# Attention, gate and channel block: 64-bit weights converted in chunks of 512 columns, with a new written order of jobs

## The chip, the cores and the metric

One core of a Trainium2 chip runs the whole block. The metric is the device time of one execution in microseconds (us). Three runs of the kernel before gave 603.58, 603.62 and 603.73 us; the median is 603.62 us. One further execution was profiled. PE is the matmul engine (PEld its weight loads), DVE the vector engine, ACT the scalar engine, POOL the GpSimd engine, SP the engine that issues most DMAs.

## What is computed

Three stages follow each other, for 2 batches of 768 tokens of 512 channels:

```
mask = bucket(q) == bucket(k)                      # hashed with a small projection
a    = softmax(where(mask, q @ k.T / 8, -1e9)) @ v # 8 heads of 64
g    = sigmoid(causal_conv5(a, conv_w)) * (a @ w_val) @ w_out
u    = g + real(fft(fft(g, axis=seq), axis=channel))
out  = u + relu(layernorm(u) @ w_ch1) @ w_ch2
```

The weights w_val, w_out, conv_w, w_ch1 and w_ch2 arrive as 64-bit floats. The kernel takes their bits apart with integer operations and makes of each number two 32-bit parts, a high and a low one, which the matmuls then use as separate products.

## The kernel before, in words

The attention works on 8 pairs of heads. Each pair has 6 query tiles for each of its two heads, so there are 96 steps, numbered n from 0. `ATTENTION` (lines 116 to 408) has one string of jobs for each step; `follow` (line 719) issues them in exactly that order, and the engines run their own instructions in the order of issue. A job's name may carry + or -, which shift the step that it belongs to: `X++` in the string of step 10 is the X of step 12. The jobs of a step are:

- C (PE, line 982): scores, 128 queries x 768 keys, into the one score bank; c (DVE, 992) clamps them into SBUF and takes a minimum.
- X (ACT, 1001): Exp; T (PE, 1012): six transposes; H (ACT, 1024) copies them as the high part; L (DVE, 1027) makes the low part.
- V (PE, 1038): product with the values; O (ACT, 1045) takes the sum out, o (SP) moves half of it across partitions, A (POOL, 1064, "xm") adds the halves.
- et, eh, el, J0, J1, S, s, z, Q0, b0 and others prepare the next pairs. P (POOL, 631 and 633) are steps of the convolution, two for each tap.
- w0 to w7 convert w_val, u0 to u7 the first chunk of w_out. In the last steps E (PE, 614) are the first products with w_val, sg0 to sg3 (ACT, 604) the sigmoids of the gate, and wm (1368) a Sigmoid of one column.

`words_split` (line 654) gives the eight steps of a conversion. a0 and g0 (DVE) mask the high word of a number; g1 joins the low word to g; a1 (ACT) rescales the exponent; a2 (DVE) puts the sign back; e0 (DVE) takes the power of two out of a; low (DVE) multiplies g by it; high (ACT) copies a. Before, a unit of work is half a chunk: 128 rows x 256 columns (`half_weights`). Words a and g lie side by side in one PSUM bank, the bank "m", and word e lies in SBUF, in the buffer "cve". Each of the 8 pairs converts one half of w_val (four chunks of 128 rows), and the last pair also converts the two halves of w_out's chunk 0. SP loads a half (256 columns of 64 bits) into one of two buffers `wvr`. Chunks 1 to 3 of w_out are converted behind the attention by `chunk` (line 1633), already by 512 columns, with a in the bank "m", g in the bank "o" and e in SBUF.

The weights of the channel stage go through another function, `from64` (line 502), by 512 columns; its words all lie in SBUF. Its lines 525, 532 and 538 are the counterparts of a0, g0 and g1.

A second list, `ORDERS` (line 37), has the order of the jobs of the stages behind the attention.

Of the kernel before, what the change touches and what calls it, by code (L numbers as in the profile page):

```python
# [10 lines left out]
F32 = mybir.dt.float32  # L11
# [3 lines left out]
I32 = mybir.dt.int32  # L15
I64 = mybir.dt.int64

P = 128
# [20 lines left out]
O8 X7a D6a X7b O9 H7a O10 Y8 L7a H7b E8 A6a st1 Y9 B6a L7b E9 st0 X8a Y10 X9a D7a st3 H8a D7b ag3 st4 A7a O11  # L39
ag0 L8a sq0 A7b ag1 ag4 H9a sq1 L9a rs0 st5 no3 E10 no0 st2 D8a ag5 Y11 ag2 B7a D9a sq2 B7b A8a rs1 X10a B8a A9a  # L40
r0 H10a E11 r3 no4 L10a D10a B9a no1 rs2 X11a r4 v0 r1 H11a w0 v3 no2 L11a D11a w3 A10a r2 v1 B10a N00 no5 w1
A11a c32 r5 c30 B11a N10 v5 c36 v4 Z00 v2 c31 w2 N01 Z10 w4 N11 P00 w5 N02 P10 st0+ Z01 N12 c33 Z11 c35 c38 I0a
c37 P01 st3+ Z12 P11 I0b st1+ h0a l0a c40 c34 c41 I1a st4+ h0b c43 c47 ag3+ ag0+ c42 sq0+ I1b c45 Z02 h1a c46
# [4 lines left out]
ur0 c54 S14 uc0 T0++ c55 tr1 ag5 T1++ S11 sq2 tc1 c60 ur1 bh0 rs2 c62 I2a bl0 c61 uc1 c66 no5 S12 c63 no2 I2b  # L48
c67 c68 h2a c64 c65 l2a c72 ta0 tr2 c70 h2b S20 tc2 l2b c71 S24 W1+ S23 c73 c76 ur2 S22 W2+ uc2 c78 c77 bh2 I3a
# [3 lines left out]
I0a td0- td2- tb1- A2 te2- td1- I0b A6 h0a th2- te1- l0a f0 F3 tl2- h0b th1- G0 f2 I1a te0- l0b A0 tl1- F1 T2+  # L53
h1a F5 f3 W6 F4 l1a A1 T3+ G2 f5 I1b f1 f4 A3
# [3 lines left out]
M5 T7 s1 F5 s3 B3- F1 U1+ B5- B8- M3 B7- B4- M7 l11 A2 U0+ G2 c12 F4 c22 h12 W1 G1 h22 W2 M4 W3 A0 F0 W4 A1 l22  # L58
""",
    """  # L60
M1 h21- U2 W5- l21- W6- G0- l12- G5- U3 s0 A6- G3- W7- M2 T0 M6 A3- c11 G4- A5- A8- A7- s1 F3 T1 A4- F2 B0- M5
T2 B1- T3 B2- M7 s3 B3- h11 T4 B5- F1 B6- F0 B7- B8- T5 F4 l11 T6 c22 M3 U4 B4- G0 A0 c12 F5 T7 h12 M4 h22 A1
# [3 lines left out]
M1 h21- l21- G4- U5- s0 l22- U6- F0 A2- A3- G3- A7- A5- G1- U7- F1 G2- A6- B0- M2 A8- A4- B1- B2- M6 c11 B3- F3  # L66
s1 B7- F2 f0 B6- M5 f2 B8- G5- f3 s3 B5- M7 f1 h11 B4- M3 c22 W0 M4 l11 A0 c12 F5 h21 A2 F4 W1 h22 f5 G2 h12 f4
""",
    """
M1 W2- l21- G0- s0 l22- A1- G1- W3- W4- F0 l12- A3- M2 W5- A6- W6- G4- A7- A8- G5- A5- W7- F1 M6 c11 A4- M5 s1  # L70
B2- B0- h11 B1- F2 l11 s3 M7 B3- B6- B5- M3 B7- B8- A0 B4- G3- A1 G2 A3 F3 c12 A5 A2 h12 F5 A7 c22 F4 l12 M4 A6
B0 A8 A4
""",
    """
M1 h21- h22- l21- G0- l22- s0 B1- B2- F2 B3- G5- W0- B5- M2 B6- G4- B7- B8- B4- G1- A2 F0 W1- F1 A6 W2- M6 A0
W3- A1 c11 G3- f1 h11 M5 s1 A3 f0 A8 F3 s3 f2 F5 W4- M3 W5- l11 W6- A7 M7 f3 A5 c12 G0 c22 h12 G2 f5 W7- F4
# [3 lines left out]
l11 A2 A3 G0 s1 l22- A5 M5 A7 A6 M7 B0 A8 A4 B1 G5- W0 s3 F3 B3 c22 F1 B5 B2 M3 F4 c12 B7 M4 h12 A0+ l12 A1+ G1  # L80
B6 F5 A3+ B8 h22 B4 G2 h21 G4 l21 A2+ G3 W1
""",
    """
M1 W2- W3- M2 s0 W4- A7 W5- F0 A6 W6- M6 l22- A8 A5 A4 F1 c11 s1 B2 G5- B0 W7- B1 M5 B6 M7 s3 f1 h11 F2 c22 F5
# [3 lines left out]
M1 B5- B7- f3- G2- A0 B4- M4- A1 l12- A2 G5- h21- A3 G1- l21- A5 A7 F2 s0 f4- G0- A6 G4- A4 A8 F0 l22- B0 F1 W0  # L88
# [5 lines left out]
A0+ f1 F3 A1+ M6 h11 f3 A2+ F2 A3+ s1 A6+ M5 A5+ A7+ A8+ f0 M7 s3 l11 A4+ M3 c22 f2 G0 c12 F4 B0+ f5 G1 B1+ B2+  # L94
h12 G2 B3+ h22
# [3 lines left out]
M5 l11 W2 W3 F4 s3 W4 A6+ M7 W5 A7+ G2 B0+ A4+ F5 B1+ M3 B2+ W6 c22 B3+ F0 B7+ G0 c12 M4 G1 h21 h22  # L99
# [18 lines left out]
T Y0 Y1 y0 H C+++ y1 X++ R+ c+++ yz  # L118
""",
    """  # L120
T r L- C+++ U- yb- H X++
""",
    """
T c++ cl-- L- X++ C+++ wl0-- V q- H D2-- c+++ wl+++++ R
""",
    """
T r- L- C+++ X++ q- V H c+++ R O
""",
    """
T r- k0-- o- L- U+++ C+++ X++ Q0 q- V H c+++ R  # L130
""",
    """
T r- L- A-- C+++ H q- V k1--- c+++
""",
    """
T O- X+ k3---- o- J0- k2---- k7---- J1- L- D0---- C+++ S- H V s- c+++ X++ z- J0 J1 L
""",
    """
T S- C+++ s- H k6----- V z- c+++ X++
""",  # L140
    """
T A--- b0-- L- O- X++ C+++ k4------
""",
    """
T w0-- H- o-- w1-- et c++ V- D1------- k5------- eh H V w2-- L- w3-- C+++ X++ k8-------
""",
    """
T A--- c++ O- et o- eh L- C+++ X++ Q1- el- H c+++
""",
    """  # L150
T et w4---- C+++ L- w7---- A-- H V- ns-- c+++ eh V el- X+++ C++++ w5---- L
""",
    """
T O- X+ o- V w6----- el- b1--- H c+++ k9----------
""",
    """
T et L- C+++ eh D0+ H V c+++ A-- X++
""",
    """
T L- C+++ O- X++ o- el- et V c+++ D1 eh  # L160
""",
    """
T H- k10------------- np- C+++ L- H V X++ A-- el- J0+ c+++ et O
""",
    """
T o- L- et C+++ Q0- eh eh- V c+++ H J1 X++ V+ el- L A- C++++ S U----- X+++ s
""",
    """
T c+++ J0 H J1
""",  # L170
    """
T O- L- z-- S- o- C+++ X++ el-- s- V D2------ c+++ H z-
""",
    """
T b0-- L- C+++ H V c+++ X++ A--
""",
    """
T L- O- C+++ o- H w0-- U--- V nr- X++ w1-- c+++
""",
    """  # L180
T w3--- et L- C+++ H A-- w4--- V eh c+++ U++
""",
    """
T O- X+ L- o- et C+++ Q1- el- eh V H w5---- nm c+++
""",
    """
T X+ et L- C+++ H ns-- el- V A-- eh c+++
""",
    """
T P0- O- X+ L- o- C+++ P0-- b1--- V H el- c+++ P0 w7------  # L190
""",
    """
T X+ w2------- D2- C+++ L- wl------- et V c+++ eh H
""",
    """
T w6-------- A--- O- et L- X+ C+++ P0 o- el- V H D0 c+++
""",
    """
T eh- X+ el- et D1- C+++ L- H V A-- c+++ eh
""",  # L200
    """
T P0- O- X+ np-- o- el- J0 C+++ L- Q0- H U+ J1 c+++
""",
    """
T S- X+ et- s- V- L- J0 H A-- C+++ eh- z- L X++ J1 V c+++ S
""",
    """
T O- s- X++ o- C+++ z-
""",
    """  # L210
T H- c++ P0--- b0-- V- L- X++ C+++ P0-- w0- wl- V H c+++ el---
""",
    """
# [2060 lines left out]
```

## Time and profile before

| | before |
|---|---|
| median of 3 runs | 603.62 us (603.58 to 603.73) |
| the profiled execution | 603.55 us |
| its span, first to last instruction | 601.7 us |
| around the span | 1.85 us |
| DVE busy | 527.4 us (88%), 1042 instructions |
| ACT busy | 377.7 us (63%), 750 instructions |
| POOL busy | 228.3 us (38%) |

The granted clock of PE is full speed (2.4 GHz) in all of the span. The attention's transposes run from 13 to 240 us; its last products end near 251 us. PE has work in nearly every microsecond from there to the end. In the views, "idle before" names the wait of an engine ahead of an instruction and what ended it; times of the timeline count from the start of the span. Matmul ends are modelled, so the weight loads tell more about gaps than the matmuls.

### The profile page before, as it was taken

What the parts mean: (1) busy time and instruction counts of PE and PEld (TensorE: products, weight loads), DVE (VectorE), ACT (ScalarE), POOL (GpSimd) and SP (SyncE); (2) the same over time, 40 slices, a digit from 0 to 9 for tenths busy, and PEclk for the clock granted to TensorE, in tenths of its full rate; (3) what the DMA queues carried; (4) which work ended last, traced back from release to release, by engine and by line L of the source; (5) the groups of instructions that cost most, each with busy time, mean ns of one, the idle gap of its engine ahead of it and who ended that gap; (6) DMA issues with size and microseconds to landing.
All of it is one profiled execution on the core that took longest, in us unless ns stands there. A gap on an engine that the chain in (4) does not pass through costs nothing.

```text
span 601.7 us, 10402 instructions
## 1 busy us (share of the span) xinstructions
PE 591.5 (98%) x3631; PEld 540.8 (90%) x3631; DVE 527.4 (88%) x1042; ACT 377.7 (63%) x750; POOL 228.3 (38%) x272
## 2 busy tenths in 40 slices
PE   8999999999999999999999999999999999999997
PEld 6889999999999989998899989999989898889886
DVE  5998999999999998799789999999999999985335
ACT  6898999998999987853636465545353443442121
POOL 7422769696989797894340310000000000000000
PEclk9999999999999999999999999999999999999999
DMA  5866686757575651144021122112232232310004
GB/s 131 210 144 138 164 203 152 191 132 180 154 164 150 176 130 45 45 177 164 1 71 36 36 71 70 36 35 71 71 96 80 70 101 76 104 36 0 2 35 175
DMA packets 54958, 62.03 MB, mean 103 GB/s; under 512 B 29184, under 2 KB 42664, under 8 KB 54650
## 3 DMA queue, kind: packets, MB, share of 16 engines
q1 hardware_dynamic: 54170, 57.81, 36.0%
q0 software_dynamic: 432, 3.55, 1.5%
q8 instruction: 29, 0.48, 0.4%
q14 instruction: 23, 0.19, 0.1%
q10 hardware_dynamic: 304, 0.01, 0.0%
HBM read 36.74 MB, written 3.19 MB: 66 GB/s over the span
## 4 chain that ended last, share of the span: by engine, by line
PE 88%; DVE 3%; POOL 3%; ACT 3%; DMA 1%; issue 1%; SPq 0%; POOLq 0%; DVEq 0%; ACTq 0%
PE acc L2139 22%; PE pf L2098 16%; PE op L1038 10%; PE sp L982 9%; PE ptp L1012 8%; PE ps L1729 5%; PE pf L1556 3%; PE ps L614 3%; PE ps L1826 2%; PE ps L1790 2%; PE bp L873 1%; PE early L614 1%; PE late L614 1%; PE ps L1556 1%; POOL g L633 1%; DVE ptl L1027 1%
## 5 line engine op out<-in xcount | busy, mean ns | idle before, releaser
L992 DVE TENSOR_SCALAR_CACHE_REDUCE sd<-sp 128x768 f32<-128x768 f32 x96 | 91.3, 951 | 5.5 <-PE sp L982 4.6
L1027 DVE TENSOR_TENSOR ptl<-ptp,pth 128x768 fp32r<-128x768 f32 x96 | 91.4, 952 | 5.0 <-ACT pth L1024 2.7
L982 PE MATMUL sp<-qk 128*128 128x512 f32 (+1 forms) x384 | 90.4, 357 | 2.2 <-DVE sd L992 1.3
L1001 ACT ACTIVATE sd<-sd,nm 128x768 f32<-128x768 f32 x96 | 90.6, 944 | 1.6 <-DVE sd L992 1.2
L1024 ACT CAST pth<-ptp 128x768 fp32r<-128x768 f32 x96 | 76.4, 798 | 5.3 <-PE ptp L1127 2.1
L1012 PE MATMUL ptp<-ident,sd 128*128 128x128 f32 x576 | 78.9, 273 | 0.7 <-ACT sd L1001 0.6
L1038 PE MATMUL op<-pth,v 128*128 128x256 f32 x288 | 74.3, 286 | 0.2 <-ACT xc L1045 0.2
L1038 PE MATMUL op<-ptl,v 128*128 128x256 f32 x288 | 73.0, 284 | 0.2 <-DVE ptl L1027 0.2
L1012 PEld LDWEIGHTS ptp<-ident,sd 128*128 128x128 f32 x576 | 65.1, 140 | 3.8 <-ACT sd L1001 1.9
L982 PEld LDWEIGHTS sp<-qk 128*128 128x128 f32 x384 | 58.5, 189 | 10.8 <-DVE sd L992 4.6
L2139 PE MATMUL acc<-vh,hid 128*128 128x512 f32 x192 | 66.7, 394 | 0.0
L1038 PEld LDWEIGHTS op<-pth,v 128*128 128x128 f32 x288 | 54.2, 188 | 3.6 <-ACT xc L1045 0.5
L1038 PEld LDWEIGHTS op<-ptl,v 128*128 128x128 f32 x288 | 54.2, 188 | 0.5 <-POOL xm L1064 0.4
L1064 POOL TENSOR_TENSOR xm<-xc,xs 64x256 f32<-64x256 f32 x48 | 35.2, 734 | 41.0 <-DMA xs<-xc 35.0
L633 POOL TENSOR_TENSOR g<-g,conv_tmp 128x768 f32<-128x768 f32 x27 | 46.6, 1727 | 1.4
L2098 PE MATMUL pf<-t,s 128*128 128x384 f32 x234 | 45.4, 336 | 0.0
L529 ACT ACTIVATE cv<-cv,col 128x512 int32<-128x512 int32 x32 | 23.1, 723 | 32.9 <-DVE cv L525 32.8
L2098 PEld LDWEIGHTS pf<-t,s 128*128 128x128 f32 x234 | 41.6, 188 | 2.0
L2139 PEld LDWEIGHTS acc<-vh,hid 128*128 128x128 f32 x192 | 36.0, 188 | 7.3 <-DVE hid L1548 0.5
L1544 ACT ACTIVATE hid<-snap 128x384 fp32r<-128x384 f32 x39 | 20.0, 523 | 33.4 <-DVE snap L2197 26.7
L2139 PE MATMUL acc<-gl,hid 128*128 128x512 f32 x144 | 38.9, 394 | 0.0
L2139 PE MATMUL acc<-w,hid 128*128 128x512 f32 x144 | 38.8, 393 | 0.0
(294 smaller groups left out, 1360.6 us busy)
## 6 DMA issues: line engine op xcount, KB each, us to landing
raw<-in_moe_w_ch_dram SPq DMA_DIRECT2D x32, 512.0 KB
qk<-ht SPq DMA_DIRECT2D x60, 192.0 KB
qk<-lt SPq DMA_DIRECT2D x30, 192.0 KB
rqk<-in_q_dram SPq DMA_DIRECT2D x16, 192.0 KB
rqk<-in_k_dram SPq DMA_DIRECT2D x16, 192.0 KB
rv<-in_v_dram SPq DMA_DIRECT2D x8, 384.0 KB
out_dram<-o SPq DMA_DIRECT2D x12, 256.0 KB
xs<-xc SPq DMA_DIRECT2D x47, 64.0 KB
```

Of the source, the lines that this page charges most:

```text
L633: nc.gpsimd.tensor_tensor(dst, dst, tmp, op=ALU.add)
L982: nc.tensor.matmul(sp[:, cs], q2[i][:, m, qi * P : (qi + 1) * P], k2[i][:, m, cs], start=m == order[0], stop=m == order[1])
L992: nc.vector.tensor_scalar(sd[n], sp, CLAMP, None, op0=ALU.min, op1=ALU.min, accum_out=st[p]["nm"][:, n % 12 : n % 12 + 1],)
L1001: nc.scalar.activation(sd[n], sd[n], AF.Exp, bias=st[p]["nm"][:, i : i + 1], scale=-1.0, accum_out=st[p]["sums"][:, i : i + 1],)
L1012: nc.tensor.transpose(tp[:, r // 3, c0 : c0 + P], sd[n][:, r * P : (r + 1) * P], ident)
L1024: nc.scalar.copy(p_part(n, "pth"), p_turned(n))
L1027: nc.vector.tensor_tensor(p_part(n, "ptl"), p_turned(n), f32(p_part(n, "pth")), op=ALU.subtract)
L1038: nc.tensor.matmul(po[kb], v3[:, r, c0 : c0 + P], pt[kb, x][:, r, :], start=r == 0 and x == "pth", stop=r == R - 1 and x == "ptl",)
L1064: nc.gpsimd.tensor_tensor(st[p]["xm"][mr, blk * QB : (blk + 1) * QB], xcs[kb][mr, :], xss[kb][mr, :], op=ALU.add)
L1729: nc.tensor.matmul(yp, x[:, c, kt * P : (kt + 1) * P], w[c], start=n == 0, stop=n == 3 * NC - 1)
L2098: nc.tensor.matmul(to, a[x][:, c, :], b_[y][:, c, :], start=not more and n == 0, stop=n == 5, skip_group_check=more,)
L2139: nc.tensor.matmul(accs[t], x[:, ts_], w, start=begin and n == 0, stop=ends(m) and n == 2)
```

## The change

The unit of a conversion becomes a whole chunk of 512 columns. Word a takes the bank "m", g takes the SBUF buffer "cve", and e is written over a; for that, `high` moves ahead of e0 among the eight steps. The pairs 0, 2, 4 and 6 convert one chunk of w_val each and the others none; w_out's chunk 0 is one unit in the last pair. `wvr` is one buffer of 512 columns, loaded four times. The core of the diff:

```
-        return [a0, g0, g1, a1, a2, e0, low, high]
-    def half_weights(raw, dst, b):
-        n = DM // 2
-        def tile_of(x):
-            t = psm.tile([P, DM], F32, tag="m", name="cvp").bitcast(I32)
-            return dict(a=t[:, :n], g=t[:, n:])
-        return words_split(raw, dst, b, tile_of)
+        return [a0, g0, g1, a1, a2, high, e0, low]
+    def word_tile(x, got):
+        if x == "e":
+            return got["a"]
+        if x == "g":
+            return ap4.tile([P, DM], I32, tag="cve", name="cv")
+        return psm.tile([P, DM], F32, tag="m", name="cvp").bitcast(I32)
...
-            wv_raw[i] = ap4.tile([P, DM // 2], I64, tag="wvr", name="wvr", bufs=2)
-            nc.sync.dma_start(wv_raw[i], w_val[c * P : (c + 1) * P, h * DM // 2 : (h + 1) * DM // 2])
+            wv_raw[c] = ap4.tile([P, DM], I64, tag="wvr", name="wvr")
+            nc.sync.dma_start(wv_raw[c], w_val[c * P : (c + 1) * P, :])
...
-            at = n + (0 if last else 7 if p == 0 else 6)
+            if p % 2:
+                return
+            at = n + (7 if p == 0 else 6)
...
-            for x in range(2):
-                put(n + (9 if x else 5), **{f"u{q}": lambda x=x, q=q: out_word(x, q) for q in range(8)})
+            put(n + 5, **{f"u{q}": lambda q=q: out_word(q) for q in range(8)})
```

`chunk` keeps its tiles and its order. All 96 strings of `ATTENTION` are written anew, and many of `ORDERS`. Where the conversions stand: before, the first half's steps stand in the strings of steps 9 to 12 and one half follows in each pair; after, the first chunk's stand in those of steps 8 to 15, the next ones in 27 to 36, 55 to 62 and 79 to 91, and w_out's in 93 to 95. The end of the list, before:

```
T P0---- c+ o---- w3----- O-- nr--- H w4----- P0--- C++ w2----- X+ w5----- V- c++ w7----- P0-- L- X++ C+++ A---- V c+++ o--
T O- L- X++ C+++ w6------ V H c+++
T u0-- A---- C+++ L- H P0--- V o-- X++ c+++
T L- u3--- C+++ O- P0--- H u4--- V c+++ X++ A---
T u1---- P0--- E L- o-- H X++ u5---- u2---- nm---- L
T u6----- V- u7----- u0- ag----
T A---- u1-- O-- u3-- E- ns-- o-- sg0 P0---- u4-- np- H- P0--- H L- V- P0-- wm- u7-- V u2-- L E xh0 ...
```

and after, from the same step 89 on:

```
T c+ H- P0---- V- wm+++++ L- X+ A---- C++ P0--- o-- H V c++ nr--- O L X++ C+++ P0--
T c++
T A---- H- w7------------- C++ P0--- o-- X+ L- V- H c++ V nm-- L C+++ O X++
T c++ A---
T H- u0---- P0---- C++ o-- sg0++ V- c++ ag--- u3---- P0-- V H L- P0--- E X+ L O u4---- A-- V+ u5---- u1---- o X++
T V+ ns- H P0--
T L- E- P0-- H u6------ np- xh0 L sg3+ A-- O E u2------ xh1 o xh2 nq- gt0 sg2+ xl2 sg1 P0- u7------ V+ V++ ...
```

## Rows read from the trace of the kernel before

**Rows 1.** The page: busy us of PE and PEld, share of the span, instructions.

```profile
PE 591.5 (98%) x3631; PEld 540.8 (90%) x3631; DVE 527.4 (88%) x1042; ACT 377.7 (63%) x750; POOL 228.3 (38%) x272
```

**Rows 2.** Busy time by stretch: length, then busy us (instructions) of each engine, clock, DMA.

```profile
15.00:50.00 35.00, 33.73 (x243) 30.19 (x243) 33.18 (x68) 30.31 (x59) 11.00 (x17) 1.00 0.75 169
50.00:220.00 170.00, 169.61 (x1278) 159.70 (x1277) 162.50 (x306) 157.18 (x322) 131.40 (x148) 1.00 0.67 166
90.00:130.00 40.00, 40.00 (x308) 38.16 (x307) 38.65 (x73) 36.93 (x76) 33.02 (x36) 1.00 0.62 156
220.00:250.00 30.00, 28.07 (x200) 26.30 (x201) 25.51 (x49) 24.27 (x49) 25.11 (x26) 1.00 0.19 51
```

**Rows 3.** Conversion steps by shape: line, engine, operands, count, busy us, mean ns, idle before.

```profile
L691 DVE TENSOR_SCALAR cv<-cvp 128x256 int32<-128x256 int32 x10 | 4.2, 417 | 0.0
L691 DVE TENSOR_SCALAR cv<-cvp 128x512 int32<-128x512 int32 x3 | 2.1, 691 | 0.1
L684 ACT ACTIVATE cvp<-cvp,col 128x512 int32<-128x512 int32 x3 | 2.0, 660 | 0.8 <-DVE cvp L671 0.8
```

**Rows 4.** Single lines, ns min/median/max; then the timeline of POOL and DVE.

```profile
L532 DVE TENSOR_SCALAR cv<-raw x32: 396/421/1514, 299.0 to 540.5; 128x512 int32<-128x512 int32 x32
L538 DVE SCALAR_TENSOR_TENSOR cv<-raw,cv x32: 681/685/1661, 299.5 to 545.2; 128x512 int32<-128x512 int32 x32
L688 DVE SCALAR_TENSOR_TENSOR cvp<-wvr,cvp x8: 419/422/425, 42.2 to 224.4; 128x256 int32<-128x256 int32 x8
...
314.65 2.77 POOL L1851 TENSOR_TENSOR u<-y 128x512 f32<-128x512 f32 x2 [0.37 <-DVE y L1837]
...
314.76 1.51 DVE L532 TENSOR_SCALAR cv<-raw 128x512 int32<-128x512 int32 x1
316.30 1.66 DVE L538 SCALAR_TENSOR_TENSOR cv<-raw,cv 128x512 int32<-128x512 int32 x1
```

**Rows 5.** The page: the convolution's addition on POOL.

```profile
L633 POOL TENSOR_TENSOR g<-g,conv_tmp 128x768 f32<-128x768 f32 x27 | 46.6, 1727 | 1.4
```

**Rows 6.** ACT's groups: the table load ahead of the first Exp.

```profile
L764 ACT ACT_TABLE_LOAD x1 | 1.3, 1283 | 2.6 <-issue 2.6
```

**Rows 7.** Timeline of ACT, last steps: start, length, line, operation.

```profile
222.04 0.94 ACT L1001 ACTIVATE sd<-sd,nm 128x768 f32<-128x768 f32 x1
222.97 0.78 ACT L1024 CAST pth<-ptp 128x768 fp32r<-128x768 f32 x1
...
239.34 0.37 ACT L1045 COPY xc<-op 128x256 f32<-128x256 f32 x1 [0.34 <-PE op L1038]
240.01 0.45 ACT L684 ACTIVATE cvp<-cvp,col 128x256 int32<-128x256 int32 x1 [0.30 <-DVE cvp L674]
240.48 1.28 ACT L604 ACT_TABLE_LOAD   x1
241.78 0.85 ACT L604 ACTIVATE g<-g 128x768 f32<-128x768 f32 x1
242.53 1.48 ACT L1024 CAST pth<-ptp 128x768 fp32r<-128x768 f32 x2
243.90 0.21 ACT L1368 ACTIVATE warm<-warm 128x1 f32<-128x1 f32 x1
```

**Rows 8.** Stretch from H88 to H95, and ACT's longest wait in the last steps.

```profile
222.97:243.91 20.94, 19.45 (x138) 17.93 (x136) 16.99 (x35) 16.62 (x34) 17.44 (x18) 1.00 0.12 36
...
ACT xc L1045 <- POOL xm L1064: 2.2, 2, 1.6
```

**Rows 9.** Timeline of the weight loads, last steps.

```profile
238.27 0.19 PEld L1038 LDWEIGHTS op<-pth,v 128*128 128x128 f32 x1
...
238.99 0.68 PEld L1012 LDWEIGHTS ptp<-ident,sd 128*128 128x128 f32 x6
...
244.35 0.65 PEld L614 LDWEIGHTS early<-xh,wvh 128*128 128x128 f32 x4 [1.12 <-DVE ptl L1027]
...
250.67 0.70 PEld L614 LDWEIGHTS late<-x,wvh 128*128 128x128 f32 x4
```

More of the change, by code (lines that the diff above doesn't have):

```diff
@@ L38 @@
     """
[L39 to L43, printed above, removed]
+O8 X7a D6a X7b O9 H7a O10 Y8 L7a H7b E8 A6a st1 Y9 B6a L7b E9 X8a st0 Y10 X9a D7a st3 H8a D7b ag3 A7a st4 O11
+ag0 L8a sq0 A7b ag1 ag4 H9a sq1 L9a rs0 st5 no3 E10 no0 D8a st2 ag5 Y11 D9a ag2 B7a sq2 B7b A8a X10a rs1 r0 A9a
+B8a H10a r3 no4 E11 L10a D10a B9a no1 rs2 X11a r4 v0 r1 H11a w0 v3 no2 L11a D11a w3 A10a r2 v1 B10a N00 no5 w1
+A11a c32 r5 c30 B11a N10 v5 c36 v4 Z00 v2 c31 w2 N01 Z10 w4 N11 P00 w5 N02 P10 st0+ Z01 N12 c33 Z11 I0a c35 c38
+c37 P01 st3+ Z12 I0b P11 st1+ h0a l0a c40 c34 c41 I1a st4+ h0b c43 c47 ag3+ ag0+ c42 I1b sq0+ c45 Z02 h1a c46
 P12 l0b c48 l1a h1b P02 l1b ag4+ st5+ rs0+ c44
@@ L399 @@
+X++
 """,
     """
-T u6----- V- u7----- u0- ag----
+T V+ ns- H P0--
 """,
     """
-T A---- u1-- O-- u3-- E- ns-- o-- sg0 P0---- u4-- np- H- P0--- H L- V- P0-- wm- u7-- V u2-- L E xh0 nq- O u5--
-xh1 A-- u6-- xh3 gt0 P0- o Z V+ zc xl1 xh2 xl0 V++ sg1 xl3 Z+ xl2 E+ zc+ A sg2+ P0 sg3+ O++ o++ gg+ A++ gt2++
-gt1+ P0+ gt3++ nm++ P1+
+T L- E- P0-- H u6------ np- xh0 L sg3+ A-- O E u2------ xh1 o xh2 nq- gt0 sg2+ xl2 sg1 P0- u7------ V+ V++ xl1 A
+Z E+ zc xl0 o++ P0 gg+ xh3 Z+ xl3 zc+ gt1+ O++ gt3++ A++ gt2++ P0+ nm++ P1+
@@ L661, in word @@
         def word(x):
-            if x == "e":
-                if x not in got:
-                    got[x] = ap4.tile([P, DM], I32, tag="cve", name="cv")[:, :n]
-                return got[x]
             if x not in got:
-                got.update(tile_of(x))
+                got[x] = place(x, got)
             return got[x]
@@ L688, in a2, with high @@
             nc.vector.scalar_tensor_tensor(a, hi, -(2 ** 31), a, op0=ALU.bitwise_and, op1=ALU.bitwise_or)
+        def high():
+            nc.scalar.copy(dst()[0], word("a").bitcast(F32))
         def e0():
@@ L696, in low @@
             )
-        def high():
-            nc.scalar.copy(dst()[0], word("a").bitcast(F32))
-        return [a0, g0, g1, a1, a2, e0, low, high]
-    def half_weights(raw, dst, b):
-        n = DM // 2
-        def tile_of(x):
-            t = psm.tile([P, DM], F32, tag="m", name="cvp").bitcast(I32)
-            return dict(a=t[:, :n], g=t[:, n:])
-        return words_split(raw, dst, b, tile_of)
+        return [a0, g0, g1, a1, a2, high, e0, low]
[5 more added lines that the diff above has]
+        return psm.tile([P, DM], F32, tag="m", name="cvp").bitcast(I32)
     def out_load(c):
@@ L1278, in pair_jobs @@
                 put(n + (0 if last else 2), np=lambda: norm_spread(p - 1))
-            at = n + (0 if last else 7 if p == 0 else 6)
-            half = []
+            if p % 2:
+                return
+            at = n + (7 if p == 0 else 6)
+            words = []
             def weights(q):
-                if not half:
-                    half.extend(val_weights(p))
-                half[q]()
+                if not words:
+                    words.extend(val_weights(p // 2))
+                words[q]()
             put(at, **{f"w{q}": lambda q=q: weights(q) for q in range(8)})
-            if not last:
-                put(at, wl=lambda: val_load(p + 1))
+            if p + 2 < NPR:
+                put(at, wl=lambda: val_load(p // 2 + 1))
         def conv_jobs():
@@ L1334, in late_turn, with out_word @@
                 val_matmul(0, 0, c, tail[c])
-            outs = {}
-            def out_word(x, q):
-                if x not in outs:
-                    outs[x] = out_half(x)
-                outs[x][q]()
+            outs = []
+            def out_word(q):
+                if not outs:
+                    outs.extend(out_first())
+                outs[q]()
             def second_split():
@@ L1633, in chunk, with place @@
         def chunk(c):
-            def tile_of(x):
+            def place(x, got):
+                if x == "e":
+                    return ap4.tile([P, DM], I32, tag="cve", name="cv")
                 pl, y = (psm, "m") if x == "a" else (pso, "o")
-                return {x: pl.tile([P, DM], F32, tag=y, name="cvp").bitcast(I32)}
-            a0, g0, g1, a1, a2, e0, low, high = words_split(
-                wo_raw[c], lambda: (wo_h[c], wo_l[c]), 4, tile_of
-            )
+                return pl.tile([P, DM], F32, tag=y, name="cvp").bitcast(I32)
+            a0, g0, g1, a1, a2, high, e0, low = words_split(wo_raw[c], lambda: (wo_h[c], wo_l[c]), 4, place)
             return [lambda: run((a0, g0)), g1, lambda: run((a1, a2, e0)), low, high]
```

246 lines of the change are left out of this document (118 added, 128 removed).

## The prediction, before the result was known

> **What bounds the kernel now.** I read the page's busy times first, then busy time by stretch, then the instructions of single lines, then the end of the attention instruction by instruction. PE is busy 98% of the span with 3631 matmuls [rows 1]. The change adds and removes none, so the end moves only if the gaps between matmuls do. A modelled "PE busy" hides gaps, so I use the weight loads (PEld), of which each matmul has one. In the densest stretch, 90 to 130 us, they are busy 38.16 of 40 us, 95.4%; in 15 to 50 us 30.19 of 35, in 50 to 220 us 159.70 of 170, in 220 to 250 us 26.30 of 30 [rows 2]. Against 95.4% that is 3.2, 2.5 and 2.3 us short: some 8 us of gaps in the attention are all that an order can win, and there is no such ceiling on what it can lose. DVE is close behind PE: 95.6% busy from 50 to 220 us [rows 2].
>
> The second list of orders, for the stages behind the attention, is written anew as well, but read engine by engine its sequences are the same before and after (the one job that moves past another, X10a past rs1, is PE's and rs1 is DVE's). I cost it at nothing.
>
> **Conversions.** Before, ten halves (eight of w_val, two of w_out's first chunk) of six DVE and two ACT steps of 256 columns; after, five chunks of the same steps at 512. A DVE step takes 417 ns at 256 columns and 691 ns at 512 with a PSUM operand [rows 3]. Ten times six of 0.42 is 25 us. After, four of the six keep a PSUM operand: 4 x 0.69. The other two change place: word g now lies in SBUF, so g0 reads and writes SBUF only, and g1 reads two SBUF tensors. The channel stage has both forms: medians 421 and 685 ns [rows 4]. So 5 x (2.76 + 0.42 + 0.69) = 19.4 us, 5.8 us less. ACT also loses ten instructions; it is the less loaded engine in all four stretches, and I cost that at nothing while DVE and PE cover it.
>
> But the two SBUF forms are not always that short: their longest are 1514 and 1661 ns, while L688, with a PSUM operand, never exceeds 425 ns in this attention [rows 4]. Both long ones lie between 314.76 and 317.96 us, and two additions on POOL fill 314.65 to 317.42: each began while one of these ran, and the second ended 0.54 us after they did, about its own length [rows 4]. I read this as waiting for POOL. POOL is idle in most of the channel stage, but busy 131 of 170 us from 50 to 220 us [rows 2], its longest frequent instruction being the convolution's addition, 1.73 us [rows 5]. At that share eight of the five g0 and five g1 should start beside a POOL instruction and wait for what is left of it; half of 1.73 is 0.86, and as others are shorter I take 0.6: 8 x 0.6 = 4.8 us, from 0 up to 10 x 1.73 = 17 us. So DVE's sum goes from 5.8 us less to 11 us more; I take 1 us less. What reaches PE differs: a saving in small steps fills DVE's own idle time, a stall lands ahead of a c or an L that PE waits for. I count a third of the saving and half of the stalls: -1.9 + 2.4, **+0.5 us**, from -1.9 (no stall) to +6.6.
>
> One wait is added: e0 writes over a, so it waits for ACT's copy "high"; behind it in DVE's queue are c and L. The order puts other DVE work between them each time; 0, or an X (0.94 us [rows 7]) each if ACT is late, at most 5 us. The bank "m" is held from a0 to low; the bit sums (J0) that need it come after low in the order: 0. SP issues four weight loads less, and the next chunk is read 17 or more steps (over 2 us each) after its load: 0.
>
> **The order up to step 88.** Nothing in the trace shows the new order. Its ends are the gaps of the first two stretches, -5.7 us, and as much the other way. In the first pair it puts fewer conversion steps ahead of step 9, but they come in by step 15; the pile on DVE moves more than it shrinks. From step 27 on, three pairs carry a whole chunk and three none. That speaks against a large gain, so I take a quarter of 5.7: **-1.5 us**.
>
> **The last steps.** Here the new order shows something that I can price. ACT's sequence before has the last Exp (X of step 95) ahead of the first Sigmoid (sg0). After, it is: H88, wm (a Sigmoid of one column), X90, H89, O, X91, H90, X92, H91, O, X93, H92, sg0, u1, H93, X94, O, u5, X95, H94, H95. The trace has a table load ahead of its first Exp and another ahead of its first Sigmoid [rows 6, 7]. If each return between the two costs a load, there are four before H95 in place of one. One takes 1.28 us, 1.30 from its start to the Sigmoid's; the instruction ahead of it ended at 240.46, the load began at 240.48 [rows 7]. Pitches from the same rows: X 0.93, H 0.69, sg0 0.75, wm 0.1; O 0.3; u1 0.57 (660 ns [rows 3] less the overlap) and u5 0.5. So 8 H + 6 X + 3 O + 4 loads + wm + sg0 + u1 + u5 = 5.5 + 5.6 + 0.9 + 5.2 + 0.1 + 0.75 + 0.57 + 0.5 = 19.1 us. Before, ACT went from the start of H88 (222.97) to the end of H95 (243.91) in 20.94 us, 16.62 of them busy and 4.3 idle [rows 7, 8].
>
> For PE, the new order pays back: V94 and V95 (0.72 us each, 238.27 to 238.99) come ahead of T95, and the 1.12 us wait for L94 at 244.35 has two E products in front of it. Before, T95 began at 238.99 and the attention's last product gave way to the next stage at 250.67 [rows 9]: 11.68 us, after 11.68 - 1.44 - 1.12 = 9.1. T95 needs X95, which ends two H before the chain does: 222.97 + 19.1 - 1.4 + 9.1 = 249.8 plus ACT's waits, against 250.67. Without waits 0.9 us are won, with the same 4.3 us 3.4 are lost; if a return to Exp costs nothing, 2.6 less at both ends. Of the 4.3 us, 2.2 were O behind xm on POOL [rows 8], and the new order puts that xm (A85) ahead of two convolution steps that it stood behind. I take 1.7 us of waits: **+0.8 us**, from -3.5 to +3.4.
>
> The Trainium skill, page "ScalarE: Activation LUTs", section "Table sets: the hidden batching unit", names exp and sigmoid as anchors of different sets and advises finishing one set before switching; no run yet shows the way back from Sigmoid to Exp. Its section "What ACT_TABLE_LOAD costs" adds a drain of about 1.38 us to each load's 1.28; the trace agrees on the load, and shows no drain in the 0.02 us ahead of it. By the page the last steps would come to +6.3 (an estimate: 4 x 1.38 more) in place of +0.8.
>
> **Sum.** +0.5 - 1.5 + 0.8 = -0.2 us on the profiled execution's 603.55 us (601.7 span and 1.85 around it; the runs' median is 603.62): 603.3 us, no change that can be told. A measurement of this kernel tells a change from none at about 0.2%, 1.2 us.
>
> **Rivals.**
> - *DVE's stalls and ACT's reloads reach PE* (slower). For it: PE and DVE are within a few per cent of each other, so a DVE stall over one step's slack passes on; ACT has 1.9 us to spare in the last steps (20.94 - 19.1). Against it: the last steps' new PE order, and PE waits for DVE in pieces of under 1 us now. It decides once ACT's waits there pass 1.7 us or eight collisions cost over 0.6 us each. Price: all of the stalls' 4.8 us without the saving, and 0.8 in the last steps, less 1.5 to 3 for the order: 606.3 us.
> - *The order closes half of the gaps* (faster): 5.7 / 2 = 2.9 us of the two early stretches, the conversions at 0, the last steps at 0: 600.7 us. For it: 3.2 us of gaps sit in the first 35 us, where conversion steps crowd DVE and are now spread wider. Against: the pile only moves.
> - *A drain at each table change* (slower): ACT empties before each of the four loads, and the chain of the last steps, whose slack is 1.9 us, grows by as much. If a drain were as long as the load, 4 x 1.28 = 5.1 us: 608.4 us. Against it is the gap of 0.02 us before the one load that can be seen [rows 7]; that instruction ahead was short, which leaves the rest of the chance. The Trainium skill's section "What ACT_TABLE_LOAD costs", named above, is the rule behind it.
>
> **Chances.** Forecast 0.42 (602 to 604.8 on its own, mostly within 0.2%: same 0.24, faster 0.13, slower 0.05); stalls and reloads 0.28 (slower 0.25, same 0.03); gaps closed 0.26 (faster 0.25, same 0.01); drain 0.04 (slower). Faster 0.38, same 0.28, slower 0.34. The range that leaves out a tenth on each side reaches to the two rivals: 600.2 to 606.3 us.
>
> **What would show it.** Right: 3631 matmuls; six DVE steps x5 at 512 columns where g0 and g1 have a spread from 0.42 to over 1.5 us while those with a PSUM operand stay at 0.69; five table loads from wm to sg3 in place of one, each of 1.28 us, with X90 and X94 behind one; PEld shares as now up to 220 us, within 1.5 us. Wrong: g0 and g1 all short (then the lower end); PEld waiting for X (ptp from ACT sd) by over 3 us from 220 us on, or PEld over 95% from 15 to 50 us.

## The result, and the profile after

The kernel after takes 610.36 us (median of 4 runs, 609.20 to 611.28) beside 603.67 us for the kernel before (4 runs, 603.58 to 605.88): ratio 1.0101, 95% interval 1.0072 to 1.0130, that is 4 to 8 us slower. The profiled execution took 609.20 us, its span is 607.4 us; it stands 5.65 us above the one of before. PE's granted clock is full (2.4 GHz) in the profiled execution for as long as PE works, and its mean over the execution 0.998; the means of the other three runs are 0.999, 0.996 and 0.997 for 610.01, 611.28 and 610.71 us, so the longest may hold some time at half clock, at a place that the record does not show.

The page of the kernel after, as [rows 1], and the busy time by stretch, as [rows 2] (length, then busy us and instructions of PE, PEld, DVE, ACT, POOL):

```profile
PE 594.7 (98%) x3631; PEld 540.6 (89%) x3631; DVE 525.7 (87%) x1012; ACT 382.2 (63%) x744; POOL 229.8 (38%) x272
```

```profile
15.00:50.00 35.00, 34.21 (x247) 30.86 (x245) 33.66 (x65) 31.27 (x62) 10.49 (x16) 1.00 0.83 186
50.00:220.00 170.00, 168.99 (x1255) 156.26 (x1254) 159.66 (x285) 153.75 (x308) 131.32 (x146) 1.00 0.65 163
90.00:130.00 40.00, 39.84 (x299) 36.87 (x298) 37.84 (x67) 36.62 (x75) 31.10 (x33) 1.00 0.60 154
220.00:250.00 30.00, 25.70 (x183) 23.40 (x182) 21.24 (x35) 27.07 (x46) 23.11 (x25) 1.00 0.11 28
```

The work is the same 3631 matmuls. PEld is busier in the first 35 us (+0.7) and less busy from 50 to 220 us (-3.4) and from 220 to 250 us (-2.9). DVE has less work, 525.7 us for 527.4: it is not busier, it stands still more.

Where the time is lost shows best in the starts of the transposes T on PE's timeline, one per step, and the start of the first "late" product (of its weight load), where the attention's products end. I use this table for every kernel below. Each column is the length of a stretch less its length before (us); the first row has the lengths of before.

| | to T0 | pair 0 | 1 | 2 | 3 | 4 | 5 | 6 | T84 to T88 | T88 to late | behind |
|---|---|---|---|---|---|---|---|---|---|---|---|
| before (lengths) | 13.24 | 32.06 | 27.97 | 28.63 | 28.00 | 28.19 | 28.38 | 27.71 | 7.82 | 28.66 | 351.07 |
| after | -0.53 | -1.90 | +2.21 | -0.41 | +0.79 | +0.30 | +0.89 | +1.04 | +0.02 | **+3.04** | +0.25 |
| new_one_load | +0.89 | -2.09 | +2.68 | -0.40 | +0.53 | +0.30 | +0.90 | +1.04 | +0.01 | **-0.69** | +0.28 |
| old_five_loads | +1.30 | -0.24 | -0.02 | +0.03 | +0.02 | -0.02 | +0.05 | +0.02 | +0.01 | **+1.76** | +0.65 |
| old_order_chunks | +0.02 | +0.61 | +0.22 | **+3.01** | +0.36 | +1.22 | +0.70 | +0.86 | +0.92 | +0.92 | +0.24 |
| old_then_new_tail | +0.72 | +0.53 | +0.24 | +2.95 | +0.33 | +1.24 | +0.69 | +0.85 | +0.92 | +2.10 | +0.21 |
| old_chunks_conv_late | -0.17 | +0.82 | +0.24 | **+1.26** | +0.36 | +1.21 | +0.72 | +0.87 | +0.92 | +0.96 | +0.35 |
| old_g_in_sbuf | -0.10 | +0.07 | +0.44 | +0.17 | +0.60 | +0.84 | +0.76 | +0.32 | +0.07 | +2.14 | +1.58 |
| old_paired_halves | -0.34 | +1.97 | +0.16 | +3.29 | +0.45 | +1.75 | +1.28 | +1.28 | +1.73 | -0.59 | +0.05 |
| new_order_halves | -0.74 | -1.28 | +3.09 | +0.24 | +2.89 | +1.83 | +0.86 | +2.23 | +0.17 | +4.58 | -0.07 |
| new_halves_to_14 | +0.87 | -1.28 | +2.03 | +0.33 | +0.13 | +0.02 | 0.00 | 0.00 | +0.02 | 0.00 | 0.00 |
| old_no_val | +1.45 | -0.12 | -0.23 | -0.03 | -0.29 | -0.21 | -0.09 | -0.04 | 0.00 | +0.08 | +0.12 |
| new_one_load_no_val | -0.42 | -1.96 | +2.21 | -0.86 | +1.38 | +0.15 | +0.50 | +0.65 | +0.01 | -0.70 | 0.00 |
| old_late_sigmoid | -0.14 | +0.15 | -0.01 | +0.09 | 0.00 | 0.00 | +0.01 | 0.00 | 0.00 | +0.04 | -0.03 |

Two things make this table usable. A stretch with the same order repeats closely in different executions: to within 0.13 us in pairs 3 to 6 of old_five_loads, new_halves_to_14 and old_late_sigmoid, less well in pair 0 (-0.24 and +0.15 with the same jobs). The time to T0 does not: it ran from 12.5 to 14.7 us, among kernels with the same first jobs too, so differences of a microsecond between whole executions can come from there.

Read so, the kernel after gains 1.9 us in the first pair, gives 2.2 back in the second, loses 2.6 more in pairs 2 to 6, and 3.0 us in the last steps. Behind the attention nothing happens, as the prediction had it. PE's waits for a clamp between 48 and 225 us (total, times, longest), after and then before:

```profile
PEld sp L974 <- DVE sd L984: 4.3, 14, 0.6
```

```profile
PEld sp L982 <- DVE sd L992: 2.0, 7, 0.6
```

The conversions' SBUF-only steps, as [rows 4] (ns min/median/max):

```profile
L668 DVE TENSOR_SCALAR cv<-wvr x4: 409/422/828, 44.4 to 201.0; 128x512 int32<-128x512 int32 x4
L668 DVE TENSOR_SCALAR cv<-wor x1: 420/420/420, 243.5 to 243.5; 128x512 int32<-128x512 int32 x1
L674 DVE SCALAR_TENSOR_TENSOR cv<-wvr,cv x4: 677/684/1109, 46.9 to 212.9; 128x512 int32<-128x512 int32 x4
L674 DVE SCALAR_TENSOR_TENSOR cv<-wor,cv x1: 680/680/680, 249.6 to 249.6; 128x512 int32<-128x512 int32 x1
```

Only two of the ten are long, by 0.41 and 0.42 us. The last steps: what PE's weight loads waited for between 224 and 262 us (total, times, longest), then ACT's timeline, as [rows 7], and PE's:

```profile
PEld op L1030 <- ACT xc L1037: 2.6, 1, 2.6
PEld ptp L1004 <- ACT sd L993: 2.5, 3, 1.2
PEld sp L974 <- DVE sd L984: 0.7, 2, 0.6
```

```profile
226.15 0.80 ACT L1016 CAST pth<-ptp 128x768 fp32r<-128x768 f32 x1
226.96 1.28 ACT L1357 ACT_TABLE_LOAD   x1
228.25 0.20 ACT L1357 ACTIVATE warm<-warm 128x1 f32<-128x1 f32 x1
228.47 1.28 ACT L993 ACT_TABLE_LOAD   x1
229.77 0.94 ACT L993 ACTIVATE sd<-sd,nm 128x768 f32<-128x768 f32 x1
...
238.57 1.28 ACT L603 ACT_TABLE_LOAD   x1
239.86 0.85 ACT L603 ACTIVATE g<-g 128x768 f32<-128x768 f32 x1
...
241.19 0.80 ACT L1016 CAST pth<-ptp 128x768 fp32r<-128x768 f32 x1
242.00 1.28 ACT L993 ACT_TABLE_LOAD   x1
243.30 0.94 ACT L993 ACTIVATE sd<-sd,nm 128x768 f32<-128x768 f32 x1
...
244.23 0.35 ACT L1037 COPY xc<-op 128x256 f32<-128x256 f32 x1
```

```profile
230.85 0.64 PEld L1004 LDWEIGHTS ptp<-ident,sd 128*128 128x128 f32 x6 [0.82 <-ACT sd L993]
...
244.63 0.19 PEld L1030 LDWEIGHTS op<-pth,v 128*128 128x128 f32 x1 [2.65 <-ACT xc L1037]
```

The stretch from the start of H88 to the end of H95, as [rows 8]:

```profile
226.15:248.47 22.32, 18.13 (x128) 16.40 (x129) 14.31 (x24) 19.97 (x33) 15.95 (x16) 1.00 0.12 31
```

H88 ends at 226.95 and T90 on PE waits for X90, which had to wait for two loads (0.82 us; T91 behind it waits another 1.25 for X91). At the second place the longest wait does not bear X's name: V94 needs the output bank that O93 empties (xc, 244.23), and O93 stands in ACT's queue behind X94 and its load. Here a reload hurt whatever was queued behind it.

### The profile page after: what moved, and what is told of

Its sections match the earlier page's. It is cut to its first block, busy times and chain, and to the rows that moved or that the text cites. A ratio compares the mean times of both kernels' runs of the same rounds, so it can differ in the third digit from the quotient of the medians.

```text
span 607.4 us, 10359 instructions
## 1 busy us (share of the span) xinstructions
PE 594.7 (98%) x3631; PEld 540.6 (89%) x3631; DVE 525.7 (87%) x1012; ACT 382.2 (63%) x744; POOL 229.8 (38%) x272
## 4 chain that ended last, share of the span: by engine, by line
PE 86%; DVE 6%; ACT 3%; issue 2%; DMA 1%; POOL 0%; SPq 0%; DVEq 0%; ACTq 0%
PE acc L2128 22%; PE pf L2087 16%; PE sp L974 10%; PE op L1030 9%; PE ptp L1004 8%; PE ps L1718 5%; PE pf L1545 3%; PE ps L613 3%; PE ps L1815 2%; DVE sd L984 2%; DVE ptl L1019 2%; PE ps L1779 2%; PE bp L865 1%; PE late L613 1%; PE ps L1545 1%
```

## Experiments

Each kernel was timed beside the kernel before; its ratio is to that. Where only jobs move, the diff shows the jobs.

**new_one_load: the table loads taken out of the kernel after.**

```
-T c+ H- P0---- V- wm+++++ L- X+ ...
+T c+ H- P0---- V- L- X+ ...
-T H- u0---- P0---- C++ o-- sg0++ V- c++ ...
+T H- u0---- P0---- C++ o-- V- c++ ...
-T L- E- P0-- H u6------ np- xh0 L sg3+ ...
+T L- E- P0-- H u6------ np- xh0 L sg0 wm- sg3+ ...
```

> The kernel after with wm and sg0 moved behind X95, just ahead of sg3: one table load in place of five, every other job where it is. Theory R (the table loads lengthen ACT's chain of the last steps, and PE waits for it): the PE waits of 2.65 us (V for O93, which stands behind X94 and its load) and of 1.25 us (T90 behind X90 and its load) shrink by at least 2.5 us together, and the kernel is 2.5 to 3.5 us faster than after: 607.0 to 607.8 us. Theory T (the order of the last steps itself is worse, loads or not): under 1 us, over 609.4 us.

Measured: 606.21 us, ratio 1.0041 (1.0028 to 1.0053), 0.6% or 3.6 us below after by the ratios, 0.8 us below the range expected. The last steps go from +3.04 to -0.69. PE's waits from 222 to 262 us:

```profile
PEld sp L780 <- DVE sd L790: 0.8, 2, 0.6
PEld op L836 <- ACT xc L843: 0.7, 1, 0.7
...
PEld ptp L810 <- ACT sd L799: 0.4, 1, 0.4
```

Theory R holds: the waits for xc and for X (sd) fall from 5.1 us to 1.1. With one load in place of five the new order of the last steps is 0.7 us better than the old one. The four loads are 5.1 us of ACT; together with the two Sigmoids that move with them (1.05 us) they cost 3.7 us of the end.

**old_five_loads: the same loads put into the kernel before.**

```
-... P0--- C++ w2----- X+ w5----- ...
+... P0--- C++ w2----- wm+++++ X+ w5----- ...
-... L- o-- H X++ u5---- ...
+... L- o-- sg0++ H X++ u5---- ...
```

> The kernel before with wm moved ahead of X90 and sg0 ahead of H93, as they stand after: five table loads in place of two, halves and the rest of the order as before. Theory R: ACT had 4.3 us of idle time between H88 and H95, the added loads take 3.8 us or more; PE ends the attention 1.5 to 3 us later: 605.1 to 606.7 us. Theory T: the old order absorbs them, under 604.6 us.

Measured: 606.84 us, ratio 1.0049 (1.0037 to 1.0061), 3.0 us; the profiled execution lost 1.76 us in the last steps, the only stretch that changed, and began 1.3 us late. PE's waits there:

```profile
PEld ptp L817 <- ACT sd L806: 3.3, 2, 1.7
PEld sp L787 <- DVE sd L797: 1.3, 2, 0.7
```

So the loads cost time in either order. The 1.76 us lie in the 1.5 to 3 expected, the median 0.14 us above its range; the old order absorbs more of the price than the new one.

**old_order_chunks: the new conversion in the old order.** The code after; the eight steps of a chunk stand where those of the even pair's half stood, the odd pairs' steps go, and the load of the next chunk moves behind the last reading of the one buffer.

> The code after (chunks of 512, g in SBUF, e over a, one wvr buffer) in the written order of before: the steps of the chunks stand in the old places of the even pairs' halves and of the first half of w_out, the odd pairs carry none. Theory O (the loss of 3.9 us from step 14 to step 88 comes from the new order): within 1 us of before, 602.7 to 604.7 us. Theory C (lumps of 0.69 us, the wait of e0 for ACT and the SBUF forms beside POOL cost it): T88 comes 2 us or more later than before and the kernel takes 605.7 us or more.

Measured: 612.93 us, ratio 1.0157 (1.0144 to 1.0170): worse than the kernel after, and T88 7.9 us later than before: what theory C expected, and against what I had come to believe from the trace of the kernel after. Pair 2 is 3.0 us longer. DVE, then POOL, then ACT there:

```profile
95.36 2.67 DVE L474 TENSOR_SCALAR cv<-wvr 128x512 int32<-128x512 int32 x1
```

```profile
95.25 0.73 POOL L862 TENSOR_TENSOR xm<-xc,xs 64x256 f32<-64x256 f32 x1
95.94 1.80 POOL L438 TENSOR_TENSOR g<-g,conv_tmp 128x768 f32<-128x768 f32 x1
...
98.94 0.94 ACT L799 ACTIVATE sd<-sd,nm 128x768 f32<-128x768 f32 x1 [2.38 <-DVE sd L790]
```

The g0 that took 0.42 us elsewhere took 2.67: it began while POOL added halves and ended 0.29 us after the convolution's addition that followed. Behind it the clamp, then X, then PE waited. Over all ten SBUF-only steps 6.1 us were lost so (2.25 here, 2.82 in u1, 0.63, 0.35 and less in others), seven times what the new order loses.

**old_chunks_conv_late: is it POOL?** Two convolution steps move on POOL's queue; nothing else moves.

```
-... T O- P0-- L- ... V X++ c+++ P0 ...
+... T O- L- ... V X++ c+++ ...
-... T O- A--- L- ...
+... T O- A--- P0---- P0-- L- ...
```

> old_order_chunks with two convolution steps of POOL (a product and an addition, 2.7 us together) moved behind the next addition of halves (A of step 31), so that POOL is idle when the g0 of the second chunk runs, near 96 us; nothing moved on DVE, ACT or PE. Theory S (g0 waits for POOL): that g0 falls from 2.67 us to 1.1 us or less, PE's wait of 2.0 us for the clamp behind it shrinks to under 0.7 us, and the pair from step 24 to 36 is 1.2 to 1.8 us shorter than the 31.64 us of old_order_chunks. Otherwise (the instruction is long for another reason): it stays over 2 us.

Measured: 611.15 us, ratio 1.0112 (1.0098 to 1.0127), 1.8 us less than old_order_chunks by the medians, 2.7 by the ratios. DVE and POOL at the same place:

```profile
95.44 0.42 DVE L474 TENSOR_SCALAR cv<-wvr 128x512 int32<-128x512 int32 x1
```

```profile
94.30 0.72 POOL L862 TENSOR_TENSOR xm<-xc,xs 64x256 f32<-64x256 f32 x1
97.11 0.74 POOL L862 TENSOR_TENSOR xm<-xc,xs 64x256 f32<-64x256 f32 x1 [2.10 <-DMA xs<-xc]
```

With POOL idle the same instruction takes 0.42 us, and pair 2 is 1.75 us shorter (29.89 for 31.64). PE's waits for clamps between 75 and 110 us, first old_order_chunks, then this kernel:

```profile
PEld sp L780 <- DVE sd L790: 3.2, 4, 2.0
```

```profile
PEld sp L780 <- DVE sd L790: 1.5, 3, 0.9
```

The longest is 0.9 us, not under 0.7 as expected: g1, 1.17 us long at 98.1, now met the moved steps. Theory S is shown for this instruction.

**old_g_in_sbuf: the SBUF forms alone.** Halves, old order; g and e change homes.

```
-            if x == "e":
+            if x == "g":
...
-            return dict(a=t[:, :n], g=t[:, n:])
+            return dict(a=t[:, :n], e=t[:, n:])
```

> The kernel before with the homes of g and e exchanged: halves, e beside a in the bank m, g in SBUF, so that g0 reads and writes SBUF alone and g1 reads two SBUF tensors, 20 such steps of 256 columns; order and number of steps as before. Theory S (stalls beside POOL, 2 of 10 such steps of 512 columns took 2.3 and 2.8 us too long in old_order_chunks): 605 to 608 us. Theory L (whole chunks in even pairs are what costs): within 0.6 us of before.

The edit also gives the three chunks behind the attention a g in SBUF, which the expectation left out; that is the +1.58 behind (one g1 there, at 259.06 us, takes 2.24 us for 0.68). Measured: 613.14 us (610.45 to 613.79), ratio 1.0135 (1.0110 to 1.0160), more than expected; the profiled execution was the fastest of them. Steps g0 and g1 of w_val (ns min/median/max):

```profile
L479 DVE TENSOR_SCALAR cv<-wvr x8: 271/522/1181, 36.3 to 226.3; 128x256 int32<-128x256 int32 x8
L485 DVE SCALAR_TENSOR_TENSOR cv<-wvr,cv x8: 408/706/1253, 37.3 to 228.1; 128x256 int32<-128x256 int32 x8
```

Against the short forms (0.28 and 0.41 us) the sixteen lose 5.8 us on DVE, and pairs 0 to 6 are 3.2 us longer: somewhat over half of a stall reaches PE (5.0 of the 5.8 fall in these pairs). The last steps lost 2.14 us, and not by stalls alone. DVE, PE's weight loads and the busy time, as [rows 2]:

```profile
239.74 3.35 DVE L485 SCALAR_TENSOR_TENSOR cv<-wor,cv 128x256 int32<-128x256 int32 x1
```

```profile
244.08 1.11 PEld L817 LDWEIGHTS ptp<-ident,sd 128*128 128x128 f32 x6 [2.12 <-issue]
```

```profile
244.16:247.57 3.41, 3.41 (x13) 3.41 (x14) 1.31 (x5) 3.00 (x5) 3.26 (x3) 0.50 0.10 24
```

A g1 of w_out stalled, PE stood for 2.1 us, and then its granted clock was at half (1.2 GHz) for 3.41 us. T95 and the two E products behind it took 3.5 us so; the same sequence at 237.8 us took 2.0 at full clock. About 1.5 of the 2.14 us are thus clock (an estimate from these rows). The five runs have mean clocks of 0.993 to 0.997, so a part of the 613.14 us that the record does not size is clock as well. The price of the SBUF forms is to be read from pairs 0 to 6, which ran at full clock.

**old_paired_halves: whole chunks without SBUF forms.** The kernel before, with the odd pair's half converted in the even pair: two steps stand wherever one stood.

> The kernel before with both halves of a w_val chunk converted in the even pair, two steps in each place where one stood, and none in the odd pair; PSUM forms and sizes as before, u as before. Theory L (DVE cannot take a whole chunk in one pair, and gets nothing back from the pair without one): 606.5 to 609 us, T88 3 to 5 us later than before. Theory S: within 1 us of before.

Measured: 614.56 us, ratio 1.0174 (1.0155 to 1.0193), twice what theory L expected. The four pairs with a chunk lose 8.3 us together, the pairs without gain nothing (+0.16, +0.45, +1.28). Part of it may be the edit's own: an ACT step of the conversion now often stands right behind the DVE step that it needs, and between 15 and 225 us ACT waits 6.7 us for such steps, before 0.5. The two largest of these waits:

```profile
ACT wvh L504 <- DVE wvl L499: 2.1, 1, 2.1
...
ACT cvp L489 <- DVE cvp L485: 1.5, 2, 0.9
```

So pairs with a whole chunk are longer in PSUM forms too; how much of the 8.3 us is the lump and how much these waits stays open.

**old_then_new_tail: the new last steps behind the old body with chunks.** The order of old_order_chunks up to T87, that of after from there.

> The code after; the order of before (with chunks as in the run old_order_chunks) up to T87, the order of after from there on with its five loads. Theories R and O together: the time of old_order_chunks plus the 3.0 us that the last steps lost, 606.2 to 607.2 us. If the last steps suffered only because DVE arrived with a backlog from the new order: within 1.5 us of old_order_chunks.

Measured: 614.70 us, ratio 1.0181 (1.0167 to 1.0196); 1.8 us above old_order_chunks by the medians, 1.2 in the last steps. Expected were 3.0 or under 1.5; the medians lie between them, the stretch under 1.5. The stretch is the better figure, since the runs' mean clocks differ (1.000 in the two shorter ones, the profiled one among them, 0.996 and 0.997 in the two longer). The tail that it replaces is itself 0.9 us worse than before; a g0 of w_out takes 3.24 us in it.

**new_halves_to_14 and new_order_halves: the new order with the old conversion.** Code before. In the second the jobs other than the conversion's stand as after (with one load) and each half step ahead of the clamp or low part that it preceded in the old order; the first follows it up to T14 and then the old order.

> The code before; the written order of new_order_halves up to T14, from there on the order of before. After had T12 2.4 us and T14 1.5 us earlier than before; half of that came with fewer conversion steps ahead of step 12, which is not so here. If the gain of the start is the order's and is kept: 602.4 to 603.1 us. If it is handed back by DVE later: 603.4 us or more.

> The code before (halves of 256 columns, a and g in one PSUM bank) in the written order after, with sg0 and wm ahead of sg3 (one load), and the half steps put ahead of the same clamp or low part as in the old order. Theory N (the new order of the other jobs is better by itself, and the chunk form takes that away): 601.0 to 602.8 us. Theory O (the new order of the other jobs is what loses up to step 88): 605 to 606.5 us, as new_one_load.

Measured: 605.09 us, ratio 1.0017 (1.0006 to 1.0027), and 617.79 us, ratio 1.0232 (1.0208 to 1.0256). The first answers the question of the start: -1.28 in pair 0, +2.03 in pair 1, +0.33 in pair 2, and then nothing; the gain is handed back with interest. The second missed both theories by far; in its last steps (+4.58) the granted clock was at half from 239.8 to 243.2 us, after weight loads that were busy for 1.9 of the 4.8 us before. It shows that steps set down in an order that was not made with them cost more than either order; it does not price the new order, and the next pair had to.

**old_no_val and new_one_load_no_val: both orders without the conversion of w_val.** Left out are the loads and conversion steps of w_val; its two parts are filled with 0.5 by POOL in the first pair.

```
-            return words_split(wv_raw[c], lambda: (wvh[:, c, :], wvl[:, c, :]), 3, word_tile)
+            if c == 0:
+                for k in range(NC):
+                    for x in (wvh, wvl):
+                        nc.gpsimd.memset(f32(x)[:, k, :], 0.5)
+            return [lambda: None] * 8
```

> The kernel before without the conversion of w_val: its loads and its eight times eight steps are left out, and both parts of w_val are filled with 0.5 by eight POOL instructions in the first pair; w_out, the order and everything else as before. 20 us of DVE work go. Theory F (an order serves the load that it was drawn up for; PE is bound in the pairs, so that work taken off DVE brings little): 600 to 603.5 us. Theory D (DVE bounds the attention as much as PE): under 599 us.

> The same taken from new_one_load: no conversion of w_val in the written order after, one table load. Theory O (the new order of the other jobs is slower by itself): 2 us or more above old_no_val. Theory C (the new order is as good, the whole chunks are what costs in new_one_load): within 1 us of old_no_val.

Measured: 602.86 us, ratio 0.9977 (0.9969 to 0.9986), and 605.03 us, ratio 1.0006 (0.9993 to 1.0019). The stretch from 50 to 220 us of each, in the same order:

```profile
50.00:220.00 170.00, 169.59 (x1287) 160.36 (x1286) 153.47 (x272) 154.99 (x311) 131.84 (x148) 1.00 0.64 157
```

```profile
50.00:220.00 170.00, 168.49 (x1260) 156.68 (x1259) 151.12 (x267) 151.84 (x304) 130.70 (x146) 1.00 0.63 156
```

Theory O holds in the main: with no conversion of w_val in either, the new order is 0.29% slower, 1.75 us (2.2 by the medians, where 2 or more was expected): 3.1 us longer in pairs 0 to 6, 0.8 shorter in the last steps. Its PEld share is as low as in the kernel after. In pairs 0 to 6 the conversions add 1.0 us to the old order (before less old_no_val) and 0.9 us to the new one (new_one_load less this kernel): chunk and halves cost about the same, each in its own order (1.4 and 2.1 us by the ratios of the whole, with intervals that overlap). And 20 us of DVE work taken away bring 1.4 us.

**old_late_sigmoid: an attempt to beat both.** The kernel before with sg0, and so its one load, behind H95.

```
-... o-- sg0 P0---- u4-- np- H- P0--- H L- V- P0-- wm- ...
+... o-- P0---- u4-- np- H- P0--- H L- V- P0-- sg0 wm- ...
```

> The kernel before with the first Sigmoid (sg0) and so the one table load of the last steps moved from ahead of H94 to behind H95. Theory R (a load on ACT's chain of the last steps reaches PE): H94 begins 2 us earlier, PE's wait of 1.12 us for L94 goes, and the kernel is 0.6 to 1.2 us faster than before. If the copies and O95, which now stand behind the load, are as urgent: within 0.4 us of before.

Measured: 603.66 us beside 603.80, ratio 0.9998 (0.9986 to 1.0011). H94 did begin 2 us earlier, at 240.50. PE's waits of the last steps, before and then in this kernel:

```profile
PEld early L614 <- DVE ptl L1027: 1.1, 1, 1.1
...
PEld rp L1086 <- POOL xm L1064: 0.2, 1, 0.2
```

```profile
PEld rp L891 <- POOL xm L869: 1.4, 1, 1.4
```

The wait for L94 went, and a wait for POOL's xm of the same size took its place. No kernel here that does the whole work beat the one before.

## Why the prediction was wrong, point by point

The forecast was 603.3 us, no change, range 600.2 to 606.3; the result lies 4 us above the range.

- **The order up to step 88 (forecast -1.5 us).** This is the step that failed, in sign: pairs 0 to 6 lost 2.9 us, and T88 came 2.4 us late. I took the missing weight loads of 15 to 50 us as time to be won. Half of my own objection was right, "the pile on DVE moves more than it shrinks": pair 0 wins 1.9 us, pair 1 pays 2.2. But I let the other half of the stretch stand at a gain, and it lost 2.6 us in pairs 2 to 6. The runs without w_val show that this is the other jobs' order: without that conversion pairs 0 to 6 are still 3.1 us longer than in the old order. In the profile after PE waits 14 times for a clamp between 48 and 225 us, 4.3 us in all, before 7 times and 2.0; seven of the 14, before one of the 7, are scores right behind the transposes of the next pair's q and k. Which displaced job makes each of them late was not taken apart.
- **Conversions (forecast +0.5 us).** The mechanism was right: steps on SBUF operands wait for POOL, which old_chunks_conv_late shows for a g0. For an order drawn without regard to it the sum came out near (about 6 us of stalls in old_order_chunks and in old_g_in_sbuf, forecast 4.8; somewhat over half of it at PE, where I counted half), partly by luck: in old_order_chunks four of ten steps stalled and not eight, and two of them lost 2.25 and 2.82 us, more than the 1.73 that I took for the longest wait. It was wrong for this order, which sets eight of ten where they run at full speed and loses 0.83 us. The whole term came to about 0. Whole chunks in every other pair, for which I had a remark but no price, go with a cost in the old order: in old_chunks_conv_late pairs 0, 2, 4 and 6 are 0.8 to 1.3 us longer, stalls included, and the pairs between them return nothing. In the new order, made for chunks, no such cost shows.
- **The last steps (forecast +0.8, bound +3.4).** Mis-sized: +3.0, of which the loads are +3.7 and the rest -0.7. The four loads were counted at their right length, 1.28 us, and the step from T95 to the end, 9.1 us, measured 9.4. The 2.2 us that I missed lie in small pieces along ACT's chain. H88 stood 0.8 us later behind T88 than before, behind X89 and O87. From the start of H88 (226.15) to the end of H95 (248.47) ACT took 22.3 us; its work was 20.0 of them and not 19.1, its idle time 2.35 and not 1.7. PE's new order did shorten the step from T95 to the end, by 2.3 of the 2.6 us that it was to pay back, but V94, now ahead of T95, waited there 2.65 us for O93.
- **The rivals.** The one on the slower side named the reloads and the stalls; the first half was the larger cause, the second hardly took place. The drain at a table change did not show: H88 ends at 226.95 and the load begins at 226.96, and X90 follows the second load by 0.02 us. The Trainium skill, page "ScalarE: Activation LUTs", section "What ACT_TABLE_LOAD costs", adds 1.38 us of drain to each load; the five loads from wm to sg3 in this trace show the 1.283 us and no drain.
- **The signs.** Of those that I named for being right, the five table loads came. The spread of g0 and g1 did not (longest 1.11 us, "over 1.5" named), and PEld lost 3.4 us from 50 to 220 us where I allowed 1.5. Of those for being wrong none appeared: PE waited for X by 2.5 us, "over 3" named.

Put together by ratios: loads 0.60% (3.6 us), order of the other jobs 0.29% (1.75 us), leaving 0.12% (0.7 us), which is inside the intervals, of the 1.01%. By the stretches of the profiled executions: loads 3.7 us, order of the other jobs 3.1 in pairs 0 to 6 less 0.8 in the last steps, conversions about 0; with the time to T0 (-0.5) and the stretch behind (+0.3) that is the 5.7 us by which the span grew.

## What to carry to other kernels

An engine's missing busy time is not a reserve that a new order can draw on: price an order by the waits that it makes, and look whether a gain in one stretch is asked back in the next. Keep functions of different activation tables apart: count each change of table at its load, and look at what is queued behind it, not only at the function that needs it. An order and the durations of its steps belong together, so a change of step sizes is judged only with an order made for it, and the order alone by leaving the changed work out on both sides.

## What the runs showed of the hardware that I had not expected

A DVE instruction on SBUF operands alone can lose to POOL twice in a row. The g0 at 95.36 us in old_order_chunks waited through the addition that was running (to 95.98) and through the next one (95.94 to 97.74), whose start came after its own; the one at 243.16 us did the same and took 3.24 us in place of 0.42. DVE, then POOL there, in old_order_chunks:

```profile
243.16 3.24 DVE L474 TENSOR_SCALAR cv<-wor 128x512 int32<-128x512 int32 x1
```

```profile
242.49 1.82 POOL L438 TENSOR_TENSOR g<-g,conv_tmp 128x768 f32<-128x768 f32 x1
244.27 1.84 POOL L952 TENSOR_TENSOR xT<-xm,rs 128x768 f32<-128x768 f32 x1
```

I had bounded one wait by one POOL instruction, 1.73 us. The Trainium skill, page "SBUF — State Buffer", section "Who interferes with whom", describes an exclusive lock that the first comer holds for its instruction; the trace agrees with the lock, but in these two cases being first in line did not get DVE the turn when POOL's instructions followed each other without a gap.

PE's granted clock fell to half in the middle of the work in two kernels, old_g_in_sbuf and new_order_halves, for 3.41 us each, right after PE had stood. In the profiled execution of the kernel after a wait of 2.65 us (ahead of V94) brought no such fall. No run shows by itself that the standing brought the fall. But the granted clock of a stretch belongs beside its length, before a stall is priced.
